# The order of SP's transfers written out by readiness, weight preparation moved to POOL, and squares taken from the moved tile

## The chip, the cores and the metric

The kernel runs on one core of one Trainium2 chip. The metric is the device time in microseconds. Three runs of the kernel before took 2990.77, 2992.46 and 3002.14 us; their median is 2992.46 us. A further, profiled execution took 2998.08 us, with a span of 2996.4 us from its first to its last instruction.

The engines are named as in the profile: PE (TensorE), PEld (its weight loads), DVE (VectorE), ACT (ScalarE), POOL (GpSimd) and SP (SyncE, which issues all transfers here). SPq is SP's instruction queue.

## The reference

Four transformer layers with a residual each, on x of 2048 rows by 512. Layers 0 and 2 are causal attention over a window of 256 keys with the weights A; layers 1 and 3 are full attention with the weights B. All have 32 heads of 16.

```python
def layer(x, wqkv, wo, windowed):
    q, k, v = heads(layernorm(x) @ wqkv)          # 32 heads of 16
    s = einsum("qd,kd->qk", q, k) * 16 ** -0.5    # for each head
    if windowed:
        s = where((i - j >= 0) & (i - j < 256), s, -1e9)
    return x + merge(softmax(s) @ v) @ wo

for windowed, w in ((True, A), (False, B), (True, A), (False, B)):
    x = layer(x, *w, windowed)
```

## The kernel before, in words

`fast_path` (line 189) holds the work. A layer is cut into four quarters of 512 rows (index `c`). Its steps are: load x, statistics and norm on DVE (`stats`, `norm`), transposes on PE (`transpose`), projections to queries, keys and values (`project`, `values`), attention, and the output projection with the residual (`wo`, or `wo_part` in layer 3).

Matrices are kept as two float16 parts, a high and a low one, so a projection of 128 columns is twelve matmuls (`mms`, line 382; the planner counts 0.222 per matmul). `project` (line 456) takes each bank of results `ps` out of PSUM as `sp`: the high part at line 479 on ACT (481 on DVE in the full layers), the low part at line 482 on DVE. Line 485 squares `ps` on ACT a second time out of PSUM; in the full layers line 487 squares the high part on POOL. The squares feed a bound on the scores that replaces the row maximum (`keys`, `queries`, `key_shift`). Queries and keys go to DRAM (`qs`, `kw`, `kf`) and are loaded back four heads (a `qd`) at a time: `load_win` (698) and `load_full` (686) load `qt`, two buffers, and `kt`, three. The eight `qd` of a quarter are the inner loop; in layer 3 the outer loop takes two `qd` at a time through all four quarters, so it has sixteen such passes.

Attention (`attn_win`, `attn_full`) makes scores on PE (line 673), exponentials on ACT (677), in the window layers the edges of the band by selects on POOL (739 and 742), and after two more steps (`flush(2)`) the products with the values on PE (717 and 749). A step of the full layers is one key tile for four heads, sixteen to a `qd`; the window layers have three to a `qd`.

`epilogue` (609) closes four heads. DVE copies the accumulator to `oe` (617), the denominators go to `lt` and the sums to `scr` in DRAM (622, 623). For every second `qd`, `reciprocals` runs later: it inverts `lt` (633), stores it (`rcp`, 635), loads the sums (`o`, 640) and the broadcast reciprocals (`r`, 641). Later still `normalised` multiplies them on DVE (644) and splits the product into `oh` (646, 647). The low part is taken on POOL in the full layers.

The weights of layer 0's projections are prepared at the start. The other five (`prep`, 338) are prepared during layer 0's attention. `maxima` (275) reduces each matrix's magnitudes over four row blocks in one DVE instruction (284); PE transposes the result (289). `scales` makes powers of two, and `parts` (319) scales each of four blocks (326, POOL), takes the high part (332, DVE for these five; 330, ACT, at the start) and the low part (333, POOL), and stores both in DRAM as `wd`. `weights` (367) loads them for each use into one of two buffers.

The order on PE is the order of the program (`manual_schedule`, line 202, names PE alone). On every other engine, SP among them, the compiler orders instructions by its own estimate of when their inputs are ready, with the order of the program as the priority. The program itself is laid out by a planner that counts a clock (`clock`, `spent`). `attention` (899) traces a step, then lets `Side` (818) put in pieces of projection, preparation and so on in proportion to the steps; line 876 aims to have them done two of its steps before the end of the quarter. A side step follows each window step and every second full step. What must come later waits in `pend` or `late` until the clock has reached a due time.

Of the kernel before, what the change touches and what calls it, by code (L numbers as in the profile page):

```python
# [188 lines left out]
def fast_path(ctx, tc, flag, a_x, a_wqkv, a_wo, b_wqkv, b_wo, out):  # L189
# [12 lines left out]
    ctx.enter_context(tc.manual_schedule(engines={mybir.EngineType.PE}))  # L202
# [5 lines left out]
    CM, DN, WT, ST, LN, pend = {}, {}, {}, {}, {}, []  # L208

    clock, DONE, ONR = [0.0], {}, {}  # L210

    def spent(us):
        clock[0] += us
        return us
# [60 lines left out]
    def maxima(ty, s, raw, ahead):  # L275
# [6 lines left out]
        if ahead:  # L282
            am = vp.tile([P, D], F32, name=f"wa{n}", tag="o")
            nc.vector.tensor_reduce(am, raw.rearrange("p k f -> p f k"), axis=AX.X, op=ALU.max,
                                    apply_absolute_value=True)
            yield
            pt = bank(f"wt{n}").rearrange("p (t f) -> p t f", f=P)
            for t in range(NHT):
                nc.tensor.transpose(pt[:, t, :], am[:, t * P:(t + 1) * P], ident)
            nc.vector.tensor_reduce(cm, pt, axis=AX.X, op=ALU.max)  # L290
            return
# [6 lines left out]
    def scales(ty, s):  # L298
# [7 lines left out]
        for v, name in ((up, "u"), (dn, "d"))[0 if s == 3 else 1:]:  # L306
            dg = vp.tile([P, NHT, P], F32, name=f"{name}g{n}", tag="oe")
# [11 lines left out]
    def parts(ty, s, raw, act):  # L319
# [3 lines left out]
        for k in range(NC + 1):  # L323
# [3 lines left out]
            if k:  # L327
# [3 lines left out]
                else:  # L331
                    nc.vector.tensor_copy(hi, r)
# [5 lines left out]
    def prep(ty, s):  # L338
        raw = load_w(ty, s)
        yield wait(14)  # L340
        for _ in maxima(ty, s, raw, True):
            yield wait(8 if s == 3 else 6)
# [24 lines left out]
    def weights(ty, s, n, t=None):  # L367

        w = wp.tile([P, NC, 2, D], F16, name=f"w{n}", tag="w", bufs=WB)
        if t is None:  # L370
            nc.sync.dma_start(w, wd[ty, s])
            return w
        nc.sync.dma_start(w[:, :, :, :P], wd[ty, s][:, :, :, t * P:(t + 1) * P])
# [46 lines left out]
    def load_x(l, c):  # L420
        xs = []
        for i in range(4):
            k = 4 * c + i
            x = vp.tile([P, D], F32, name=f"x{l}_{k}", tag="x", bufs=XB)
            nc.sync.dma_start(x, a_x[0, k * P:(k + 1) * P, :] if l == 0 else xd[k])
            xs.append(x)
# [29 lines left out]
    def project(l, s, c, act, w=None, ht=None):  # L456
# [3 lines left out]
        if not w:  # L460
            w = weights(ty, s, n, ht)
            yield wait(8)
        xc = XC[l, c]
# [7 lines left out]
        for t in range(NHT) if ht is None else (ht,):  # L471
# [3 lines left out]
            settle(not sqs)  # L475
            sp = vp.tile([P, 2, QC], F16, name=f"sp{n}_{t}", tag="sp", bufs=3)
# [7 lines left out]
            if act:  # L484
                nc.scalar.activation(sq, ps, AF.Square, scale=e)  # L485
# [4 lines left out]
            d = dst[8 * t:8 * t + 8].rearrange("h (d b) n -> (h d) b n", b=4)  # L490
            if s:
                nc.sync.dma_start(d[:, 0:2], sp[:, 0:1].broadcast_to([P, 2, QC]))
                nc.sync.dma_start(d[:, 2], sp[:, 1])
            else:
                nc.sync.dma_start(d[:, 0:2], sp)
                nc.sync.dma_start(d[:, 2], sp[:, 0])
# [25 lines left out]
    def queries(l, c, act, w=None, ht=None):  # L522
        sqs = yield from project(l, 0, c, act, w, ht)

        def rest():
            ph = squares(f"q{l}_{c}_{ht}", sqs)

            m = vp.tile([P, QC], F16, name=f"m{l}_{c}_{ht}", tag="m", bufs=1)
# [7 lines left out]
            for t in sqs:  # L536
                nc.sync.dma_start(rows(qs[l % 2, c])[8 * t:8 * t + 8, 3, :], m[32 * t:32 * t + 8, :])
# [6 lines left out]
    def key_shift(l, ht=None):  # L544
# [4 lines left out]
        nc.vector.tensor_reduce(kx[r], KM[l][r], axis=AX.X, op=ALU.max)  # L549
        m = vp.tile([P, QC], F16, name=f"mk{l}_{ht}", tag="m", bufs=1)  # L550
        nc.vector.tensor_scalar(m[r], ones[r], kx[r], -0.515, op0=ALU.mult, op1=ALU.mult)
        for t in range(NHT) if ht is None else (ht,):
            nc.sync.dma_start(rows(kf)[8 * t:8 * t + 8, 7, :].rearrange("h (c n) -> h c n", n=QC),
                              m[32 * t:32 * t + 8, None, :].broadcast_to([8, NQ, QC]))

    def values(l, c, act, w=None):
        n = f"{l}_{c}"
        if not w:
            w = weights(l % 2, 2, f"v{n}")
            yield wait(8)  # L560
        xc = XC[l, c]
# [13 lines left out]
    def wo(l, c):  # L575

        w = weights(l % 2, 3, f"o{l}_{c}")
        yield wait(8)

        xs = load_x(l, c)  # L580
        for i in range(4):
# [5 lines left out]
            nc.vector.tensor_add(xs[i], xs[i], d)  # L587
            nc.sync.dma_start(xd[k], xs[i])
            stats(l + 1, c, i, xs[i])
            yield -MM if PH["full"] else -12 * MM  # L590

    def wo_part(c, t):
# [6 lines left out]
        for i in range(4):  # L599
# [5 lines left out]
            nc.vector.tensor_add(xs[i], xs[i], d)  # L605
            nc.sync.dma_start(out[0, k * P:(k + 1) * P, :] if t == NHT - 1 else xd[k], xs[i])
            yield -MM

    def epilogue(l, c, qd, a, act):
        n = f"{l}_{c}_{qd}"  # L610
        t, u = divmod(qd, 2)
        oe = vp.tile([P, QC], F32, name=f"oe{n}", tag="oe")
# [5 lines left out]
        if u == 0:  # L618
            EP["scr"] = dp.tile([8, 32, QC], F32, name=f"scr{n}", tag="scr", bufs=4)
# [483 lines left out]
```

## Time and profile before

| what | value |
|---|---|
| median of three runs | 2992.46 us |
| profiled execution | 2998.08 us, span 2996.4 us |
| DVE, POOL and ACT busy in 85 to 600 us (most of layer 0) | 268.71, 248.82 and 260.98 us |
| transfers issued by SP | 395.92 MB |
| exponentials (line 677) | 2432 instructions, 1109 ns mean |

The stages: the first weights and projections up to some 85 us, layer 0 (window) to about 614 us, layer 1 (full) to about 1610, layer 2 (window) to about 2015, layer 3 (full) to about 2967, and the last output rows.

In a row of the timeline stand start, duration, engine, line, operation, and the tiles written and read. Brackets at the end hold the idle time of the engine before it and what ended that. In a row of waits stand the engine and line, what it waited for, the total, the number of times and the longest. In a row of groups: busy time and mean nanoseconds, then the idle time just before. A program with 16 DMA engines behind one issuing engine has two delays to a transfer: SP may not come to its instruction, and the data takes time to land.

### The profile page before, as it was taken

Reading aid. Unit: us, or ns where it says so; the run is one execution under the profiler, and the core shown is the slowest. Engines: PE = TensorE matmul, PEld = TensorE weight load, DVE = VectorE, ACT = ScalarE, POOL = GpSimd, SP = SyncE. Lnnn points to the kernel's source line nnn. Section 1 sums busy time; section 2 is a strip of 40 time slices with the busy share of each in tenths; the row PEclk is TensorE's granted clock in tenths of the full one; section 3 lists DMA queues with packets and bytes.
Section 4 is the critical chain, followed back from the end, with each engine's and each line's share of the span. In section 5 each row is a group of like instructions: output and inputs, shape, how many; then the busy total and the mean of one; then the engine's idle time right before and its main releaser. Section 6 shows DMA issues by size and latency. Waiting matters only on the chain.

```text
span 2996.4 us, 51979 instructions
## 1 busy us (share of the span) xinstructions
PE 2757.5 (92%) x20314; PEld 751.0 (25%) x20314; DVE 895.1 (30%) x1866; ACT 2402.0 (80%) x2703; POOL 557.5 (19%) x1127
## 2 busy tenths in 40 slices
PE   6787898899999999999999888789999999999996
PEld 3233333321122112212222333331211221112111
DVE  7665544401112113111212545531221222122212
ACT  3454555389999999999997666429999999999996
POOL 2546554100000000000002566500000000000000
PEclk8899999999999999999999999889999999999998
DMA  6575675532223232222323656432343333433332
GB/s 223 194 240 195 208 226 178 171 108 97 77 87 102 94 104 93 96 84 88 108 88 124 211 188 184 147 117 84 123 128 127 120 120 128 129 121 121 119 113 68
DMA packets 291408, 399.34 MB, mean 133 GB/s; under 512 B 70352, under 2 KB 173264, under 8 KB 283856
## 3 DMA queue, kind: packets, MB, share of 16 engines
q1 hardware_dynamic: 291152, 395.92, 40.6%
q8 instruction: 161, 2.64, 0.4%
q14 instruction: 95, 0.78, 0.1%
HBM read 263.19 MB, written 131.60 MB: 132 GB/s over the span
## 4 chain that ended last, share of the span: by engine, by line
PE 65%; ACT 10%; DVE 9%; DMA 9%; issue 4%; POOL 2%; SPq 1%; ACTq 0%; DVEq 0%; POOLq 0%
PE acc L717 25%; PE s L673 18%; PE acc L387 9%; ACT e L677 9%; PE pq L387 4%; PE pv L387 4%; DMA r<-rcp 4%; DMA rcp<-lt 3%; PE po L387 2%; PE acc L749 2%; DVE xh L417 1%; DMA scr<-oe 1%; DVE o L644 1%; DVE xh L414 1%; DVE xn L414 1%
## 5 line engine op out<-in xcount | busy, mean ns | idle before, releaser
L677 ACT ACTIVATE e<-s 128x1024 f32<-128x1024 f32 (+2 forms) x2432 | 2244.8, 1109 | 184.1 <-PE s L673 179.2
L717 PE MATMUL acc<-e,vt 128*17 128x512 f32 x8192 | 1078.6, 598 | 3.1 <-DVE oe L617 3.0
L673 PE MATMUL s<-qt,kt 64*128 64x512 f16 (+3 forms) x5504 | 798.7, 357 | 83.7 <-ACT e L677 14.2
L673 PEld LDWEIGHTS <-kt 64*128 64x128 f16 x5504 | 218.9, 94 | 944.9 <-issue 915.6
L742 POOL TENSOR_SCALAR_AFFINE_SELECT e<-e 128x256 f32<-128x256 f32 x512 | 223.7, 444 | 209.1 <-ACT e L677 208.4
L617 DVE COPY oe<-acc 128x512 f32<-128x512 f32 x128 | 88.1, 688 | 516.2 <-PE acc L717 461.9
L647 POOL TENSOR_TENSOR oh<-o,oh 128x512 f16<-128x512 f32 x32 | 37.1, 1159 | 1079.8 <-DVE oh L646 1079.8
L717 PEld LDWEIGHTS acc<-e,vt 128*17 128x17 f32 x8192 | 136.4, 95 | 351.1 <-issue 323.9
L739 POOL TENSOR_SCALAR_AFFINE_SELECT e<-e 128x256 f32<-128x256 f32 x448 | 194.3, 439 | 143.1 <-ACT e L677 140.6
L387 PE MATMUL pq<-xc,w 128*128 128x512 f16 x816 | 198.3, 397 | 12.6 <-ACT e L677 5.6
L749 PE MATMUL acc<-e,vt 128*17 128x384 f32 (+2 forms) x2816 | 204.3, 400 | 1.3 <-POOL e L739 1.1
L387 PEld LDWEIGHTS <-w 128*128 128x128 f16 x1152 | 106.2, 100 | 250.3 <-issue 157.8
L644 DVE TENSOR_TENSOR o<-o,r 128x512 f32<-128x512 f32 x64 | 53.2, 832 | 368.2 <-DMA r<-rcp 368.0
L387 PE MATMUL po<-wo,oh 128*128 128x512 f16 x444 | 113.9, 413 | 46.0 <-DVE dx L586 29.3
L479 ACT ACTIVATE sp<-pq,es 128x512 f16<-128x512 f32 x68 | 46.7, 687 | 108.6 <-PE pq L387 82.6
L387 PE MATMUL pv<-wv,xc 128*128 128x512 f16 x576 | 131.8, 385 | 1.5 <-ACT sq L485 0.6
L487 POOL TENSOR_TENSOR sq<-sp 128x512 bf16<-128x512 f16 x28 | 29.1, 1039 | 558.9 <-DVE sp L481 558.9
L387 PEld LDWEIGHTS <-oh 128*128 128x128 f16 x768 | 69.2, 101 | 213.3 <-issue 138.8
L570 ACT ACTIVATE vt<-pv 128x512 f32<-128x512 f32 x52 | 31.1, 597 | 110.1 <-PE pv L387 110.1
L387 PEld LDWEIGHTS <-xc 128*128 128x128 f16 x768 | 70.5, 99 | 140.7 <-issue 70.0
L481 DVE TENSOR_SCALAR sp<-acc,es 128x512 f16<-128x512 f32 x28 | 21.0, 750 | 268.2 <-PE acc L387 247.8
L387 PE MATMUL acc<-xc,w 128*128 128x512 f16 x336 | 95.4, 386 | 3.7 <-DVE sp L482 3.7
(128 smaller groups left out, 1486.3 us busy)
## 6 DMA issues: line engine op xcount, KB each, us to landing
kt<-kf SPq DMA_DIRECT2D x128, 512.0 KB
qt<-qs SPq DMA_DIRECT2D x128, 256.0 KB
scr<-oe SPq DMA_DIRECT2D x128, 256.0 KB
xd<-x SPq DMA_DIRECT2D x96, 256.0 KB
x<-xd SPq DMA_DIRECT2D x96, 256.0 KB
w<-wd SPq DMA_DIRECT2D x22, 1024.0 KB
kt<-kw SPq DMA_DIRECT2D x64, 256.0 KB
o<-scr SPq DMA_DIRECT2D x64, 256.0 KB
```

The source lines that it names most:

```text
L387: nc.tensor.matmul(ps, a, b, start=(i == 0), stop=(i == len(pairs) - 1))
L414: norm1 = lambda o: nc.vector.tensor_scalar(o, xs[i], mv[:, i, 0:1], y[:, i:i + 1], op0=ALU.subtract, op1=ALU.mult)
L479: nc.scalar.activation(sp[:, 0], ps, AF.Copy, scale=e)
L617: nc.vector.tensor_copy(oe, a)
L644: nc.vector.tensor_tensor(o, o, r, ALU.mult)
L647: (nc.gpsimd if l % 2 else nc.vector).tensor_tensor(ohl[:, 1], o, ohl[:, 0], ALU.subtract)
L673: nc.tensor.matmul(ps[:, h, s0:s0 + wd_], kt[R * h:R * h + R, pr, kc:kc + P], qt[R * h:R * h + R, pr, qc:qc + wd_], start=True, stop=True)
L677: nc.scalar.activation(e[:, :, w0:w1], ps[:, :, w0:w1], AF.Exp, scale=SCALE)
L717: nc.tensor.matmul(a[32 * h:32 * h + DH + 1, :], V[l, j // 4][:, j % 4, 4 * qd + h, :], es_[h // 2][:, h % 2, :], start=(j == 0), stop=(j ...
L739: nc.gpsimd.affine_select(v, v, pattern=[[0, 2], [-1, P]], compare_op=ALU.is_gt, fill=0.0, base=0, channel_multiplier=1)
L742: nc.gpsimd.affine_select(v, v, pattern=[[0, 2], [1, P]], compare_op=ALU.is_ge, fill=0.0, base=0, channel_multiplier=-1)
L749: nc.tensor.matmul(a[32 * h:32 * h + DH + 1, q * P:(q + nb) * P], V[l, (4 * c + j) // 4][:, j % 4, 4 * qd + h, :], es_[h // 2][:, h % 2, s ...
```

## The change

SP joins PE in `manual_schedule`: its transfers enter the queue in the order of the program. So that this order follows readiness, most of them are no longer issued where they are written. `post` puts a transfer on a list with a due time, the clock plus a delay, and `run_posts` issues what is due, sorted by due time, whenever the clock moves. `need` issues at once the listed transfers that write a named destination, ahead of a transfer or instruction that reads it. `number` does the same for transfers that read a tile's old buffer when the buffer is to be used again.

```diff
-    ctx.enter_context(tc.manual_schedule(engines={mybir.EngineType.PE}))
+    ctx.enter_context(tc.manual_schedule(engines={mybir.EngineType.PE, mybir.EngineType.SP}))
...
+    def post(out_, in_, delay, dst=None, of=None):
+        serial[0] += 1
+        posts.append((clock[0] + delay, serial[0], out_, in_, dst, of))
+        run_posts()
+
+    def run_posts(test=lambda x: False):
+        go = sorted(x[:2] for x in posts if x[0] <= clock[0] or test(x))
+        by = {x[:2]: x for x in posts}
+        for k in go:
+            x = by[k]
+            posts.remove(x)
+            nc.sync.dma_start(x[2], x[3])
+
+    def need(*dst):
+        run_posts(lambda x: x[4] in dst)
+
+    def number(tag, bufs):
+        made[tag] = made.get(tag, 0) + 1
+        run_posts(lambda x: x[5] is not None and x[5][0] == tag and x[5][1] <= made[tag] - bufs)
+        return tag, made[tag]
+
     def spent(us):
         clock[0] += us
+        run_posts()
         return us
```

The delays, in units of the planner's clock: weight loads 1.5; the stores of `sp` 2.5 and 3.5 (for queries the single row block first); the bound's rows `m` 2.5; key shifts 1.5; stores of x 3.0 (2.5 in layer 3); `lt` and `scr` 2.0; `rcp` 1.5; `r` 4.0; `qt` and `kt` 1.0. In the full layers the second half of `kt` waits 17 units more when the four heads before were of the same pass. `reciprocals` is due 5 after the epilogue (4.5 before) and `normalised` 9 after that (8 before). The loads of x and of `o` are issued where they stand. The loads for a pass's first four heads are posted at its start, and `need` issues them right ahead of the first scores:

```diff
+        need(("qs", 1, c), ("kf",))
+        early = KL.get("n") == (l, c, qd - 1)
+        KL["n"] = (l, c, qd)
+        post(qt, qs[1, c][pair].rearrange("r p n -> p r n"), 1.0, ("qt", n))
...
-            nc.sync.dma_start(kt, kf[pair, :, v * S // 2:(v + 1) * S // 2].rearrange("r p n -> p r n"))
+            post(kt, kf[pair, :, v * S // 2:(v + 1) * S // 2].rearrange("r p n -> p r n"),
+                 1.0 + 17 * v * early, ("kt", n, v))
...
     def attn_full(l, c, qd, kt, qt, a):
+        need(("qt", f"{l}_{c}_{qd}"))
         for j in range(NT):
+            if j % 8 == 0:
+                need(("kt", f"{l}_{c}_{qd}", j // 8))
...
-            nc.sync.dma_start(r, rcp[:, None, :].broadcast_to([8, DH, QC]))
+            post(r, rcp[:, None, :].broadcast_to([8, DH, QC]), 4.0, ("r", l, c, t))
 
             def normalised():
+                need(("rcp", l, c, t))
+                need(("r", l, c, t))
```

In the preparation of the five later matrices the high part moves from DVE to POOL, and the maxima are taken in two halves, with a planned wait of 4 between pieces (6 or 8 before) and into another buffer:

```diff
-            am = vp.tile([P, D], F32, name=f"wa{n}", tag="o")
-            nc.vector.tensor_reduce(am, raw.rearrange("p k f -> p f k"), axis=AX.X, op=ALU.max,
-                                    apply_absolute_value=True)
-            yield
+            am = vp.tile([P, D], F32, name=f"wa{n}", tag="dn", bufs=2)
+            for h in range(2):
+                f = slice(h * D // 2, (h + 1) * D // 2)
+                nc.vector.tensor_reduce(am[:, f], raw[:, :, f].rearrange("p k f -> p f k"), axis=AX.X, op=ALU.max,
+                                        apply_absolute_value=True)
+                yield
...
-                    nc.vector.tensor_copy(hi, r)
+                    nc.gpsimd.tensor_copy(hi, r)
                 nc.gpsimd.tensor_tensor(lo, r, hi, ALU.subtract)
```

In `project`, where ACT takes the high part, ACT squares that part instead of the bank:

```diff
             if act:
-                nc.scalar.activation(sq, ps, AF.Square, scale=e)
+                nc.scalar.activation(sq, sp[:, 0], AF.Square)
```

More of the change, by code (lines that the diff above doesn't have):

```diff
@@ L341, in prep @@
         for _ in maxima(ty, s, raw, True):
[L342 removed]
+            yield wait(4)
         yield -spent(1.0)
@@ L648, in normalised @@
                 ONR[l, c, t] = clock[0] + 4
-            late.append((clock[0] + 8, normalised))
-        late.append((clock[0] + 4.5, reciprocals))
+            late.append((clock[0] + 9, normalised))
+        late.append((clock[0] + 5, reciprocals))
     def run_late(done=False):
```

74 lines of the change are left out of this document (46 added, 28 removed).

## The prediction

> **What bounds the kernel now.** I read the page's first part, then the busy time by stage, then PE's gaps in the timeline of each stage, and behind each gap the engine that PE waited for.
>
> ```profile
> span 2996.4 us, 51979 instructions
> PE 2757.5 (92%) x20314; PEld 751.0 (25%) x20314; DVE 895.1 (30%) x1866; ACT 2402.0 (80%) x2703; POOL 557.5 (19%) x1127
> ...
> 85.00:600.00 515.00, 438.14 (x3466) 184.15 (x3467) 268.71 (x549) 260.98 (x342) 248.82 (x528) 0.93 0.62 201
> 600.00:1610.00 1010.00, 981.93 (x6954) 208.79 (x6953) 169.84 (x379) 953.92 (x1032) 47.75 (x47) 1.00 0.28 93
> 1610.00:2015.00 405.00, 337.96 (x2975) 139.10 (x2974) 190.94 (x433) 215.21 (x267) 194.93 (x482) 0.92 0.55 172
> 2015.00:2967.00 952.00, 937.44 (x6657) 189.72 (x6660) 195.13 (x358) 944.82 (x1024) 45.48 (x42) 1.00 0.36 116
> ```
>
> The columns of the stage rows are stage, length, busy time of PE, PEld, DVE, ACT and POOL, granted clock, DMA share and GB/s. The two full-attention layers (600 to 1610 and 2015 to 2967) have nothing to give: PE is idle 28 of 1010 us in one, ACT 7 of 952 us in the other. What can move is in the two window layers, where PE is idle 77 of 515 us and 67 of 405 us and its clock falls to 0.93 and 0.92. There the question is what PE waits for.
>
> ```profile
> 125.88 0.40 PE L673 MATMUL s<-qt,kt 64*128 64x256 f16 x2 [3.70 <-DVE km L519]
> 142.20 0.44 PE L673 MATMUL s<-qt,kt 64*128 64x384 f16 x2 [3.71 <-ACT sq L485]
> 212.01 1.09 PE L289 MATMUL wt<-ident,wa 128*128 128x128 f32 x4 [5.51 <-DVE wa L284]
> 229.77 2.75 PE L387 MATMUL po<-wo,oh 128*128 128x512 f16 x12
> 240.44 4.84 PE L387 MATMUL po<-wo,oh 128*128 128x512 f16 x12 [6.39 <-DVE dx L586]
> 251.58 4.40 PE L387 MATMUL po<-wo,oh 128*128 128x512 f16 x12 [4.77 <-DVE dx L586]
> 367.81 4.31 PE L387 MATMUL po<-wo,oh 128*128 128x512 f16 x12 [5.47 <-DVE dx L586]
> ...
> 121.06 4.17 DVE L332 CAST w<-wr 128x512 f16<-128x512 f32 x3 [1.55 <-POOL wr L326]
> 139.41 1.36 DVE L332 CAST w<-wr 128x512 f16<-128x512 f32 x1 [2.26 <-POOL wr L326]
> ```
>
> A bracket holds the idle time before the row and what ended it. In five gaps (all but the one at 212.01) DVE was in the casts of the weight preparation, line 332, waiting for POOL's products between them; what PE wanted (km, sp for the squares, dx) was queued behind. The five are 3.70 + 3.71 + 6.39 + 4.77 + 5.47 = 24.04 us. PE also comes back slow: the twelve matmuls that take 2.75 us at 229.77 take 4.84, 4.40 and 4.31 us behind three of them, 5.3 us more. So the casts cost **29.3 us**, all in layer 0.
>
> **The change part by part.** All sums are against the profiled execution, 2998.08 us with a span of 2996.4; the median of the runs shown is 2992.46, 5.6 lower. I carry the differences over to the median.
>
> *Weights on POOL alone.* Twenty casts leave DVE and twenty copies of the same shape join POOL.
>
> ```profile
> L332 DVE CAST w<-wr 128x512 f16<-128x512 f32 x20 | 26.8, 1369 | 14.1 <-POOL wr L326 14.1
> L326 POOL TENSOR_TENSOR wr<-wr,wd 128x512 f32<-128x512 f32 x20 | 26.9, 1364 | 1.2 <-ACT wd L317 1.2
> ...
> 141.95 0.41 POOL L742 TENSOR_SCALAR_AFFINE_SELECT e<-e 128x256 f32<-128x256 f32 x1
> 244.58 0.59 POOL L739 TENSOR_SCALAR_AFFINE_SELECT e<-e 128x256 f32<-128x256 f32 x1
> 370.72 0.40 POOL L739 TENSOR_SCALAR_AFFINE_SELECT e<-e 128x256 f32<-128x256 f32 x1
> ...
> 134.41 1.93 ACT L677 ACTIVATE e<-s 128x1024 f32<-128x1024 f32 x2
> 232.97 1.94 ACT L677 ACTIVATE e<-s 128x1024 f32<-128x1024 f32 x2 [2.40 <-PE s L673]
> 361.26 1.94 ACT L677 ACTIVATE e<-s 128x1024 f32<-128x1024 f32 x2 [2.40 <-PE s L673]
> 256.42 1.94 ACT L677 ACTIVATE e<-s 128x1024 f32<-128x1024 f32 x2 [8.76 <-PE s L673]
> 260.83 1.93 ACT L677 ACTIVATE e<-s 128x1024 f32<-128x1024 f32 x2
> ```
>
> The trace has no copy of this shape on POOL. One input over 256 columns takes a select 0.41 us, so 512 take at least some 0.8; two inputs over 512 take 1.36. I take 1.0, nearer the one-input end. That is 20 us more on POOL (16 to 27). What is hidden: PE uses an exponential two steps after ACT makes it, and a step with side work takes 4.4 us (256.42 to 260.83). What is late next: the selects. Those for the exponentials of 134.41 start at 141.95, of 232.97 at 244.58, of 361.26 at 370.72, each behind POOL's share of the preparation. If the copies that belong to the same weights (eight, six and four) stand in front too, they start at about 150, 250.6 and 374.7; PE without its old gaps wants them at 143.2, 241.8 and 370.1. It waits 6.8 + 8.8 + 4.6 = 20 us there in place of 29.3. **Gain 10** (from 29, if the copies fit between the selects, to a loss of 11, if all 27 us lie on the path, which leaves 29 - 27 = 2, and DVE is held up twice more by a busier POOL, 6.3 us each as below).
>
> ```profile
> 1872.76 7.05 DVE L644 TENSOR_TENSOR o<-o,r 128x512 f32<-128x512 f32 x1 [3.71 <-DMA r<-rcp]
> 1880.39 0.77 DVE L647 TENSOR_TENSOR oh<-o,oh 128x512 f16<-128x512 f32 x1
> ```
>
> A product of two SBUF tiles that takes under 0.8 us elsewhere took 7.05 us here, while selects ran on POOL back to back. The Trainium skill, page "SBUF — State Buffer", section "Who interferes with whom", says why it may be: DVE's second SBUF input comes through a port pair shared with GpSimd, and whichever starts first holds it for its whole instruction. The same rule would explain casts of 1.37 us, and it speaks on both sides: the moved copies stop fighting DVE's casts, and lengthen the time in which DVE's products and differences are blocked. By it alone the term could lie anywhere between the two ends above; the sum stays with the rows.
>
> *Maxima in two halves.* The gap at 212.01 is a reduction of 3.61 us that PE's transposes wait for. Halved, other DVE work can pass between; the transposes follow the second half, at a later due time. I take **4** of the 5.5 us; nothing excludes 0.
>
> *Squares from the moved first part.*
>
> ```profile
> ACT sq L485 <- DVE sp L482: 28.7, 19, 5.1
> PE s L673 <- ACT sq L485: 8.2, 7, 3.7
> PE phk L504 <- ACT sq_h L485: 2.1, 1, 2.1
> ...
> L485 ACT ACTIVATE sq<-pq,es 128x512 bf16<-128x512 f32 x68 | 47.1, 693 | 38.2 <-DVE sp L482 38.1
> ```
>
> ACT's square now waits until DVE has read the same bank, and holds the bank for another 0.69 us. From sp it needs ACT's own copy only, and the bank is free when DVE is done. Each time PE waited for a square (seven times before scores, and eight more in smaller rows of both layers, the last of them before phk) it may go on up to 0.69 us earlier: 15 x 0.69 = 10, of which one is counted with the casts. ACT's 38 us of waiting goes too, but ACT is not the limit there. The square itself reads SBUF instead of PSUM: no row for it, I take the same 0.69. **Gain 8** (0 to 14).
>
> *The order of SP's queue.* Here the trace shows the cause of waits, not the new order.
>
> ```profile
> DVE o L644 <- DMA r<-rcp: 368.0, 61, 11.3
> ...
> 316.91 4.16 PE L387 MATMUL pq<-xc,w 128*128 128x512 f16 x12 [1.81 <-ACT sq L485]
> 1894.35 5.28 PE L387 MATMUL po<-wo,oh 128*128 128x512 f16 x12 [7.85 <-DVE dx L586]
> 1926.85 4.44 PE L387 MATMUL pq_h<-xc,w_h 128*128 128x512 f16 x12 [2.86 <-DVE xc L450]
> ...
> 1893.00 0.69 DVE L644 TENSOR_TENSOR o<-o,r 128x512 f32<-128x512 f32 x1 [6.27 <-DMA r<-rcp]
> ```
>
> DVE stands still 368 us before the normalisation until the broadcast reciprocals land. In the full layers PE does not notice. In the window layers seven gaps of PE, from 316.91 to 1926.85, have such a stall right in front (6.27 us at 1893.00 ahead of PE's 7.85): 24 us, with 8 us of slow restarts. The change posts r four units after rcp, so SP no longer stands in front of it, and traces the normalisation 1.5 units later in all; DVE's work can pass if the compiler's order follows. Against that, r itself is issued no earlier. I take a third, **gain 10** (0 to 32).
>
> The price: SP now runs in the order of the program. The loads of a quarter's first four heads are written at the quarter's start and forced out right before its first scores.
>
> ```profile
> 2045.92 0.38 SPq L690 DMA_DIRECT2D qt<-qs  x1
> 2076.37 0.62 SPq L622 DMA_DIRECT2D lt<-oe  x1
> ...
> 2977.13 0.61 SPq L641 DMA_DIRECT2D r<-rcp  x1
> 2980.67 0.69 DVE L644 TENSOR_TENSOR o<-o,r 128x512 f32<-128x512 f32 x1 [7.71 <-DMA r<-rcp]
> ```
>
> In the kernel before, that load is issued as soon as it can be: this qt of layer 3's second quarter goes out at 2045.92, and the first quarter's last heads, still running then, are only stored at 2076.37, some 5 us after the second begins; a lead of about 25 us. 256 KB take 3.5 us from issue to use (2977.13 to 2980.67); qt with 512 KB of kt I put at 4.4 us, an estimate from that row. That is hidden if SP is over 4.4 us ahead of PE. The side work of a quarter is planned to end two of its steps early, about 7 us in a full layer and 5 to 9 in a window layer; less 2.5 us until the last store is due, SP has about 4.5 us. The 20 starts in full layers I take as hidden, and of the 8 in window layers, where side work runs late, two uncovered: **loss 8** (0 to 28 x 4.4 = 123). Weight loads, stores and x loads are posted when they can run; I count them at nothing, since the side work has 1.5 to 4 units of slack, and at the same 4.4 us a time if it has not.
>
> **Sum**: -10 - 4 - 8 - 10 + 8 = -24 us; 2998 - 24 = 2974 for the profiled execution, **2968 us** against the median.
>
> **The rivals.**
> *The order is worth more.* All of the 32 us at the r stalls goes and no start of a quarter waits: -24 - 22 - 8 = -54, **2938**. For it: the stall is in nearly every normalisation, 61 of 64. Against: r has the same three transfers in a row.
> *POOL takes it all back.* The copies sit on the path and the order changes nothing: 0 - 4 - 8 + 8 = -4, **2988**. For it: at 141.95 and 244.58 selects already stand behind the preparation. The lock that the Trainium skill's page tells of, above, would help it.
> *Slower: the first loads of each quarter come too late.* In all 28 starts PE stands until qt and kt have landed, 4.4 us less SP's lead. The other terms save 32, so it decides against the change from 28 x (4.4 - lead) = 32, a lead of 3.3 us, and costs over 0.5% from a lead of 2.7 on (47 us). At a lead of 2 it is 67 - 32 = +35: **3027**; at 2.5, **3014**. For it: in before the same loads go out some 25 us early, and in program order any late store ahead of them delays them. Against: two scores' tiles are stored up for ACT, and the side work has the two steps.
>
> **How the numbers follow.** Forecast 0.42, more from the order 0.17, POOL takes it back 0.16, slower 0.25. About 0.5%, 15 us, is what a measurement of this kernel can tell from no change. Faster by more: 0.17 and nearly all of the forecast, 0.58; within: 0.17; slower: 0.25. The range is 2932 to 3014: it leaves out half of the slower case and a little of the best.
>
> **What would show it.** Right: no casts on DVE in layer 0's preparation and twenty POOL copies of 0.8 to 1.4 us; PE's gaps before dx, km and squares of 120 to 370 us replaced by shorter waits for selects; fewer and shorter DVE waits for r in the window layers; full layers as long as before. Wrong: waits of PE's scores for qt or kt where a quarter begins, most of all 16 of them in the last layer; a layer 0 that is no shorter; DVE waits for r as long as now, which would mean that the compiler's order did not follow.

## The result, and the profile after

The changed kernel takes 3024.43 us (median of four runs, 3021.35 to 3026.68) against 2993.31 for the kernel before (four runs): ratio **1.0096** [1.0079, 1.0114], some 29 us slower (the two medians lie 31 us apart). 2968 was forecast, with a range that ended at 3014.

The engine line and the costliest group of PE, from the page of the kernel after:

```profile
span 3019.6 us, 51979 instructions
...
PE 2756.6 (91%) x20314; PEld 748.2 (25%) x20314; DVE 892.0 (30%) x1851; ACT 2399.6 (79%) x2703; POOL 571.4 (19%) x1147
...
L722 PE MATMUL s<-qt,kt 64*128 64x512 f16 (+3 forms) x5504 | 793.8, 358 | 112.5 <-DMA kt<-kw 43.2
```

PE works as long as before (2756.6 us, 2757.5 before); what grew is its idle time. The two stretches of the window layers (columns as before; they begin and end at the same times as before, though the layers moved), then the products with the values of the two window layers before and after, which give the layers' own length:

```profile
85.00:600.00 515.00, 425.80 (x3386) 175.19 (x3386) 268.59 (x521) 254.17 (x333) 262.68 (x548) 0.91 0.62 205
...
1610.00:2015.00 405.00, 339.40 (x3069) 134.82 (x3068) 185.83 (x425) 231.29 (x283) 196.88 (x486) 0.93 0.53 170
```
```profile
L749 PE MATMUL acc<-e,vt x1408: 272/379/847, 88.1 to 542.4; 128*17 128x384 f32 x63, 128*17 128x128 f32 x57, 128*17 128x256 f32 x56
L749 PE MATMUL acc<-e,vt x1408: 272/379/847, 1617.1 to 1941.7; 128*17 128x384 f32 x64, 128*17 128x256 f32 x56, 128*17 128x128 f32 x56
```
```profile
L807 PE MATMUL acc<-e,vt x1408: 272/390/847, 89.8 to 563.7; 128*17 128x384 f32 x62, 128*17 128x128 f32 x58, 128*17 128x256 f32 x56
L807 PE MATMUL acc<-e,vt x1408: 272/390/844, 1641.4 to 1968.2; 128*17 128x384 f32 x64, 128*17 128x256 f32 x56, 128*17 128x128 f32 x56
```

Layer 0 went from 454.3 to 473.9 us, layer 2 from 324.6 to 326.8. Of the 23.2 us between the two spans, layer 0 alone holds 19.6. Layer 2 is only 2.2 us longer, although PE waits 15.2 us there for late loads (4.25, 7.49 and 3.44 us, below): the change gains something in that layer too. What PE waits for, over the whole kernel, in the view of waits (total, times, longest):

```profile
PE s L722 <- DMA kt<-kw: 43.2, 10, 7.5
...
PE po L419 <- DVE m_None L573: 15.8, 1, 15.8
PE acc L807 <- POOL e L797: 13.5, 8, 6.6
...
PE s L722 <- DMA kt<-kf: 6.7, 12, 1.2
```

Before, PE waited for no kt from kw. Of the 43.2 us after, 6.42 stand at the very first scores (86.68 us), where PE before waited 5.46 us for qt; they are no loss of the change. Where the larger others are, in the timeline of PE: at the second four heads of layer 0, and then at the first scores of a quarter. Each window layer has three quarters behind its first; five of the six starts stand here, the sixth comes next.

```profile
104.22 0.82 PE L722 MATMUL s<-qt,kt 64*128 64x384 f16 x4 [5.50 <-DMA kt<-kw]
198.26 1.03 PE L722 MATMUL s<-qt,kt 64*128 64x128 f16 x8 [6.83 <-DMA kt<-kw]
339.98 0.61 PE L722 MATMUL s<-qt,kt 64*128 64x128 f16 x8 [2.97 <-DMA kt<-kw]
458.06 1.03 PE L722 MATMUL s<-qt,kt 64*128 64x128 f16 x8 [3.34 <-DMA kt<-kw]
...
1807.70 0.61 PE L722 MATMUL s<-qt,kt 64*128 64x128 f16 x8 [4.25 <-DMA kt<-kw]
...
1916.97 0.61 PE L722 MATMUL s<-qt,kt 64*128 64x128 f16 x8 [3.44 <-DMA kt<-kw]
```

The first qt of each of these five starts on SP's queue:

```profile
193.31 0.38 SPq L228 DMA_DIRECT2D qt<-qs  x1
...
335.63 0.41 SPq L228 DMA_DIRECT2D qt<-qs  x1
...
453.17 0.40 SPq L228 DMA_DIRECT2D qt<-qs  x1
...
1801.36 0.38 SPq L228 DMA_DIRECT2D qt<-qs  x1
...
1911.34 0.38 SPq L228 DMA_DIRECT2D qt<-qs  x1
```

The start of the second quarter of layer 2, with SP's queue in front of it, first after, then the same start before:

```profile
1712.69 0.84 PE L807 MATMUL acc<-e,vt 128*17 128x384 f32 x8
1712.87 0.62 SPq L228 DMA_DIRECT2D r<-rcp  x1
...
1713.55 0.96 SPq L228 DMA_DIRECT2D kw<-sp  x2
...
1714.61 0.58 SPq L228 DMA_DIRECT2D lt<-oe  x1
...
1715.82 0.39 SPq L228 DMA_DIRECT2D qt<-qs  x1
...
1721.02 1.04 PE L722 MATMUL s<-qt,kt 64*128 64x128 f16 x8 [7.49 <-DMA kt<-kw]
```
```profile
1681.35 0.41 SPq L703 DMA_DIRECT2D qt<-qs  x1
...
1689.99 0.39 PE L673 MATMUL s<-qt,kt 64*128 64x128 f16 x4
```

Before, SP issues qt 8.6 us ahead of the scores (1681.35 to 1689.99). After, PE has nothing left at 1713.5, SP is still at r, the stores and lt, and qt goes out at 1715.82: 2.3 us after PE needed it. PE starts 5.2 us after that issue. At the six starts the issue lies between 2.3 us behind and 2.2 us ahead of the moment at which PE has nothing left (1.9 behind, 1.4 and 1.6 ahead in layer 0; 2.3 behind, 2.1 and 2.2 ahead in layer 2), and PE starts 4.4 to 6.3 us after it.

The longest single gap of PE in layer 0 stands behind one instruction. DVE, POOL and PE after:

```profile
262.42 16.30 DVE L693 TENSOR_TENSOR o<-o,r 128x512 f32<-128x512 f32 x1 [4.44 <-DMA r<-rcp]
...
278.03 0.96 POOL L800 TENSOR_SCALAR_AFFINE_SELECT e<-e 128x256 f32<-128x256 f32 x1
...
280.70 1.86 PE L419 MATMUL po<-wo,oh 128*128 128x512 f16 x4 [15.77 <-DVE m_None L573]
```

A product that takes 0.69 us elsewhere lasted until POOL, busy throughout, paused; the output projection stood behind it for 15.77 us.

### The profile page after: what moved, and what is told of

The parts are those of the page before. It is cut to its first block, busy times and chain, and to the rows that moved or that the text cites. A ratio compares the mean times of both kernels' runs of the same rounds, so it can differ in the third digit from the quotient of the medians.

```text
span 3019.6 us, 51979 instructions
## 1 busy us (share of the span) xinstructions
PE 2756.6 (91%) x20314; PEld 748.2 (25%) x20314; DVE 892.0 (30%) x1851; ACT 2399.6 (79%) x2703; POOL 571.4 (19%) x1147
## 4 chain that ended last, share of the span: by engine, by line
PE 65%; DMA 11%; DVE 9%; ACT 7%; issue 3%; SPq 2%; POOL 2%; ACTq 0%; DVEq 0%; POOLq 0%
PE acc L775 25%; PE s L722 17%; PE acc L419 9%; ACT e L726 7%; PE pq L419 4%; PE pv L419 3%; PE acc L807 3%; DMA r<-rcp 3%; DMA kt<-kf 3%; DMA rcp<-lt 2%; PE po L419 2%; DMA kt<-kw 1%; SPq L228 1%; DMA scr<-oe 1%; DVE o L693 1%
## 5 line engine op out<-in xcount | busy, mean ns | idle before, releaser
L722 PE MATMUL s<-qt,kt 64*128 64x512 f16 (+3 forms) x5504 | 793.8, 358 | 112.5 <-DMA kt<-kw 43.2
L661 DVE COPY oe<-acc 128x512 f32<-128x512 f32 x128 | 88.2, 689 | 595.9 <-PE acc L775 493.7
L807 PE MATMUL acc<-e,vt 128*17 128x384 f32 (+2 forms) x2816 | 214.8, 410 | 13.6 <-POOL e L797 13.5
L693 DVE TENSOR_TENSOR o<-o,r 128x512 f32<-128x512 f32 x64 | 64.8, 1012 | 327.9 <-DMA r<-rcp 324.8
```

Of the source, the lines that this page charges most:

```text
L661: nc.vector.tensor_copy(oe, a)
L693: nc.vector.tensor_tensor(o, o, r, ALU.mult)
L722: nc.tensor.matmul(ps[:, h, s0:s0 + wd_], kt[R * h:R * h + R, pr, kc:kc + P], qt[R * h:R * h + R, pr, qc:qc + wd_], start=True, stop=True)
L807: nc.tensor.matmul(a[32 * h:32 * h + DH + 1, q * P:(q + nb) * P], V[l, (4 * c + j) // 4][:, j % 4, 4 * qd + h, :], es_[h // 2][:, h % 2, s ...
```

## The experiments

Each time is compared with the kernel before, run in turn on the same chip (3002 to 3004 us in these runs; a ratio of 0.001 is 3 us). Kernels are compared with each other by these ratios. Layer lengths are those of the profile, one or two for each kernel, from first to last product with the values.

### The parts alone

**e1_squares**: before, with `activation(sq, sp[:, 0], AF.Square)` as in the change.

> The kernel before with the squares of line 485 taken from the moved high part, nothing else. Every theory expects a small gain: the prediction's 8 us, so a ratio of 0.997 (0.995 to 1.000) against the kernel before, and no wait of PE for ACT's squares.

Measured: 1.0013 [1.0001, 1.0025], a loss of 4 us, though the interval almost reaches 1; the gain that every theory expected is not there. The waits of PE for DVE's low part, and the same place in e1 and in before:

```profile
PE s L673 <- DVE sp L482: 21.7, 8, 4.6
```
```profile
313.43 0.69 ACT L479 ACTIVATE sp<-pq,es 128x512 f16<-128x512 f32 x1 [1.28 <-PE pq L387]
...
314.92 0.63 ACT L485 ACTIVATE sq<-sp 128x512 bf16<-128x512 f16 x1
...
316.72 0.76 DVE L644 TENSOR_TENSOR o<-o,r 128x512 f32<-128x512 f32 x1 [5.35 <-DMA r<-rcp]
...
318.76 0.74 DVE L482 SCALAR_TENSOR_TENSOR sp<-pq,es,sp 128x512 f16<-128x512 f32 x1
319.55 0.71 PE L673 MATMUL s<-qt,kt 64*128 64x128 f16 x6 [4.62 <-DVE sp L482]
```
```profile
312.80 0.40 PE L673 MATMUL s<-qt,kt 64*128 64x128 f16 x4 [0.21 <-DMA kf<-sp]
...
315.40 0.74 DVE L482 SCALAR_TENSOR_TENSOR sp<-pq,es,sp 128x512 f16<-128x512 f32 x1
```

The square is early now, but the bank is not free: DVE's low part stands behind the normalisation, which waits for r. Before, the next scores ran at 312.80 without that bank and the next projection waited 1.81 us for it (row of 316.91 above); in e1 the scores are what takes it, and PE waits 4.62 us. The wait passed from ACT to DVE and from a projection to the scores.

**e2_prep**: before, with the preparation as changed (copies on POOL, maxima in halves, waits of 4).

> The kernel before with the preparation part alone: high part on POOL, maxima in two halves, waits of 4. Theory 'late first loads' (the change loses its time at the starts of the window layers' quarters, and the preparation gains as predicted): 10 to 25 us faster, ratio 0.992 to 0.997. Theory 'POOL' (the longer preparation on POOL holds back selects and blocks DVE's products of two tiles, as the 16.3 us product at 262 us of the changed kernel shows): no gain, ratio 0.999 to 1.005, with single DVE products of over 5 us in 100 to 400 us.

Measured: 0.9971 [0.9957, 0.9985], 9 us gained, at the edge of the first theory's range. No product in layer 0 lasts over 3 us. **e5_act**: the same, with the copies on ACT.

```diff
-                    nc.gpsimd.tensor_copy(hi, r)
+                    nc.scalar.activation(hi, r, AF.Copy)
```

> The kernel before with the preparation's part of the change (maxima in halves, shorter planned waits) and the twenty copies on ACT instead of POOL. With the copies on POOL this part alone had measured 0.9971, some 9 us gained, where the casts on DVE had cost 29.3 us. Theory 'POOL takes most of it back': the copies in front of the selects are what ate the rest, so here PE's waits for POOL's selects (20.8 us in 14 waits with the copies on POOL) fall back to under 8 us and the ratio is 0.990 to 0.995, 2964 to 2978 us on a chip where the kernel before takes 2993. Theory 'the gaps were only moved' (DVE was late anyway, ACT gets 20 more instructions of some 0.6 us in a stage in which its exponentials are needed): 0.996 to 1.000, and PE waits for ACT in place of POOL.

Measured: 0.9960 [0.9947, 0.9973]. Waits of PE in e2, then in e5:

```profile
PE acc L751 <- POOL e L741: 20.8, 14, 8.1
```
```profile
PE s L675 <- ACT e L679: 24.6, 42, 5.7
...
PE acc L751 <- POOL e L741: 2.9, 7, 1.0
```

The wait for the selects falls as the first theory said (20.8 to 2.9 us), and the wait for ACT's exponentials takes half of its place (14.8 us in 37 waits in e2). The two intervals overlap: which engine makes the copies is worth little.

**e3_order**: after, with squares and preparation as before, so the order of SP's queue alone.

> The changed kernel with squares and preparation put back, so SP's order alone. Theory 'late first loads': 20 to 35 us slower than before, ratio 1.007 to 1.012, with waits of PE for kt of some 35 us in the window layers. Theory 'POOL': within 8 us of before, ratio 0.997 to 1.003.

Measured: 1.0117 [1.0095, 1.0139], 35 us lost: the order, with its list and its later due times, is the loss. Kt again leads the new waits, 40.2 us in 12.

### First loads, and who orders SP

**e4_early**: after, with a window quarter's first loads written as soon as its keys and queries are projected.

```diff
-                ops = load(l, c, qds[0])
+                ops = KL.pop("first", None) or load(l, c, qds[0])
...
+                            if (qd == qds[-1] and c + 1 < NQ and "first" not in KL and not pend
+                                    and all((x, l, c + 1) in DONE for x in "KQ")):
+                                KL["first"] = load(l, c + 1, qds[0])
```

> The changed kernel, but in the window layers the loads for a quarter's first four heads are posted as soon as its keys and queries are projected, during the last four heads of the quarter before. Theory 'late first loads': 25 to 35 us less than the changed kernel, about 2990 us, and no wait of PE for kt at six of the eight starts. Theory 'POOL': at most 10 us less than the changed kernel, 3014 or more.

Measured: 1.0015 [0.9998, 1.0032], 24 us better than after, just short of what the first theory gave, and some waits at the starts stay. Kt's waits halve (7.0 of what is left is at the very first scores), and DVE's long product is not there, at the place where it was:

```profile
PE s L722 <- DMA kt<-kw: 23.9, 6, 7.0
```
```profile
261.91 0.69 DVE L693 TENSOR_TENSOR o<-o,r 128x512 f32<-128x512 f32 x1 [2.67 <-DMA r<-rcp]
```

So e4 took away two things, the late loads by its edit and the 15.8 us by its timing. **e6_free** leaves everything as changed but the order: `manual_schedule(engines={mybir.EngineType.PE})`.

> The changed kernel with one thing undone: SP is not in the manual order, so the compiler orders SP's transfers by its own estimate again, with the new order of the program as its priority. All postponed transfers, the later due times of reciprocals and normalisation, the preparation and the squares stay as changed. Theory 'late first loads, because SP runs in program order': the waits of the scores for kt and qt at the starts of quarters are nearly gone (kt of the window layers from 43.2 us to under 12), and the ratio to the kernel before is that of preparation and squares together, 0.996 to 1.001. Rival 'the postponement itself': the posts come late in the program, the compiler's order follows the program, and the later due times of the normalisation cost too: the waits stay above 30 us and the ratio is 1.007 to 1.012.

Measured: 1.0021 [1.0008, 1.0033], 22 us better than after, just above the range of the first theory and far below the rival's, and kt is gone from the larger waits. **e13_post** is e6 with the squares from PSUM again.

> The changed kernel with SP's order left to the compiler and the squares taken from PSUM again; the list of due times, the later due times of the normalisation and the preparation on POOL stay. With the squares as changed it had 1.0021; preparation alone 0.9971, squares alone 1.0013. Theory 'the parts add up, and the later places in the program cost some 11 us': 1.0008. Theory 'the order costs only because it is fixed': then with the compiler's order only the preparation is left, 0.996 to 0.998, and squares cost more beside the later due times than alone.

Measured: 0.9974 [0.9962, 0.9985], as e2's 0.9971. The list of due times and the later normalisation cost nothing, and gain nothing, as long as the compiler orders SP; squares cost 14 us there (0.9974 to 1.0021), not 4. The parts do not simply add. This tests the list only under the compiler's order, where DVE waits for r in the window layers as long as before (141.7 us, 133.8 before).

**e12_prog**: before, with SP in `manual_schedule` and nothing else.

> The kernel before with one thing changed: SP in the manual order, its transfers in the order in which the program of the kernel before writes them, with no list of due times. Theory 'a fixed order of SP makes loads late, and the list of due times repairs most of it': stores are written right after the step that makes their data, so SP stands in front of each, loads behind them come later than in the changed kernel, and it is slower than 1.012 (the fixed order with the list of due times alone): 1.015 to 1.08. Rival 'the list itself makes the loads late': without it the loads are written early and the ratio is under 1.010.

Measured: 1.0369 [1.0344, 1.0395], 111 us lost. The list repairs some two thirds of what a plain program order costs.

### What else the fixed order costs

**e14_nosq** is after with the squares from PSUM, **e9_early_nosq** the same with early first loads, **e15_again** after once more.

> The changed kernel with one thing undone: the squares are taken from PSUM again. If squares cost 14 us wherever they stand (1.0021 against 0.9974 with the compiler's order): 1.0049. If the sum of the parts alone holds (order 1.0117, preparation 0.9971): 1.0088. If squares cost nothing under a fixed order: 1.0096.

> The changed kernel with the window layers' first loads written early and the squares taken from PSUM again; preparation as changed. Chain of single steps so far: preparation 0.9971, with the list of due times and the compiler's order of SP 0.9974, with the squares 1.0021, with SP's order fixed 1.0096, with early first loads 1.0015. Theory 'late first loads are the whole cost of the fixed order, and the squares cost 14 us wherever they stand': 0.996 to 0.998, as good as the preparation alone. Rival 'the fixed order has a second cost of some 11 us that the squares only hid': 1.000 to 1.003 (the kernel with copies on ACT instead had 1.0028).

> The changed kernel once more, for a second profile. If the product of 16.3 us on DVE in layer 0, with PE's 15.8 us gap behind it, belongs to this kernel's timing, it is there again at about 262 us, at 10 us or more; if it is chance, the longest such product is elsewhere or under 4 us, and the profiled time is some 10 us shorter than 3021. The late first loads of the window quarters (6.8, 3.0, 3.3, 7.5, 4.3 and 3.4 us) are there in either case, within 1.5 us each.

Measured: e14 1.0096 [1.0062, 1.0131], e9 1.0038 [1.0018, 1.0058], e15 3032.43 us in its one run (3002.48 before). e9 lies above both ranges that were given for it, nearer to the rival's. Between after and e14 the squares cost nothing. In e15 all six late starts are there again, each within 0.6 us. The long product is in all three; e15's row, and the gap of PE behind it:

```profile
261.63 15.46 DVE L693 TENSOR_TENSOR o<-o,r 128x512 f32<-128x512 f32 x1 [4.95 <-DMA r<-rcp]
...
279.16 3.15 PE L419 MATMUL po<-wo,oh 128*128 128x512 f16 x7 [15.49 <-DVE m_None L573]
```

It lasts 16.16 us in e14 and 15.36 in e9: it belongs to this timing and is not chance. It is not the fixed order's alone: with the compiler's order it lasts 12.79 us in e6 and 11.25 in e13. There PE stands 7.78 and 7.03 us behind it, against 15.90 in e9, so under the fixed order that gap is some 8 to 9 us longer. **e17_after_act** shortens it in the changed kernel by copies on ACT (diff as e5), **e18_early_act** does that and early first loads; **e8_best** is e18 with the squares from PSUM.

> The changed kernel with one thing else: the twenty copies of the preparation on ACT instead of POOL, so that POOL pauses for each. In four profiles with the copies on POOL and SP's order fixed to the list, one DVE product of layer 0 lasted 15.4 to 16.3 us, while POOL worked 17 us without a pause, and PE stood 15.5 to 16.3 us behind it. Theory 'the unbroken run of POOL is the second cost': no DVE product over 8 us, no gap of PE for m_None, waits of the scores for kt still 40 us or more, and the ratio falls from 1.0096 by about 16 us to 1.003 to 1.006. Rival 'PE's other waits fill the place': the gap goes, ACT's copies cost as much, and the ratio is 1.008 to 1.011.

> The changed kernel with early first loads and with the copies on ACT, squares as changed: both costs that the profiles show are taken away. With early first loads alone it had 1.0015, and there the long product was absent already (0.7 us) while PE waited 16.3 us for POOL's selects. Theory 'late first loads and POOL's run are the whole loss': 0.996 to 1.000. Rival 'a fixed order costs more than these two': 1.001 to 1.004, as the same kernel with the squares from PSUM had (1.0028).

> The changed kernel with the window layers' first loads written early (as in the run with early first loads, 1.0015 against the kernel before), the squares taken from PSUM again (their part alone had measured +4 us) and the twenty copies on ACT. Theory 'late first loads', with the parts adding up: 1.0015 less 0.0013 for the squares, less what the copies on ACT gain over those on POOL (0 to 20 us): 0.994 to 1.000. Theory 'POOL': the copies are the main loss, and the ratio falls to 0.992 or lower. If the parts do not add up it stays at 1.001 to 1.003.

Measured: e17 1.0074 [1.0049, 1.0098], e18 1.0005 [0.9988, 1.0022], e8 1.0028 [1.0011, 1.0044]. In e17:

```profile
265.37 5.09 DVE L693 TENSOR_TENSOR o<-o,r 128x512 f32<-128x512 f32 x1 [4.55 <-DMA qs<-sp]
...
272.36 4.13 PE L419 MATMUL po<-wo,oh 128*128 128x512 f16 x12 [5.58 <-DVE m_None L573]
```

The waits for kt stay (41.7 us). PE's gap falls by 10 us (15.8 to 5.6), the time by 7, between the two theories, and the intervals of after and e17 overlap. Also, with copies on ACT two new waits of PE for DVE's low part appear in layer 0 (5.90 us at 149.12 and 4.70 at 253.51), so e17 does not take out the gap alone, and its price is not settled. Early first loads, in three pairs that differ in nothing else, are worth 24 us (after and e4), 17 (e14 and e9) and 21 (e17 and e18). In two pairs with early first loads that differ only in the squares (e9 and e4, e8 and e18), the changed squares are 7 us the better, though the intervals of each pair overlap.

**e11_soon** is e4 with no delay on the window layers' loads of qt and kt and on all weight loads (`post(..., 0.0, ...)`).

> The kernel with early first loads (1.0015 against the kernel before) with one thing more: the window layers' loads of qt and kt and all weight loads enter SP's queue with no delay (1.0 and 1.5 units in the change). Of the order's cost of some 35 us about 11 is left there, and PE still waits 23.9 us for kt in the window layers, 5 to 7 us of it at each of three places in layer 0, and 2 to 2.5 us for the output weights three times. Theory 'what is left are also late loads': these waits fall to under 12 us together and the ratio is 0.997 to 1.000. Rival 'it is the later due times of the normalisation and the stores in front': the waits stay and the ratio is 1.001 to 1.004.

Measured: 1.0048 [1.0031, 1.0064], 10 us worse than e4 and above both ranges. The waits in the window layers did not go (25.9 us), and new ones came in the full layers, where e4 had 9.0 us in 13:

```profile
PE s L722 <- DMA kt<-kf: 20.6, 15, 3.0
```

### DVE beside POOL, by itself

**e7_port**, **e10_port2** and **e16_port3** leave out the whole computation and time single DVE instructions of 128x512 while POOL works without a pause. In e7 the compiler ordered POOL, so its runs became selects and products in turn; in the others the order is fixed.

> Leaves out the whole computation: it copies x to the output and times single DVE instructions of 128x512 alone and beside back-to-back runs of POOL instructions on other tiles (24 or 48 selects, 8 products of two SBUF tiles, 16 copies to float16). Theory 'a DVE product of two SBUF tiles does not come in between two POOL instructions' (as the 16.3 us product in layer 0 of the changed kernel suggests): the product lasts about as long as the POOL run beside it, 10 us or so beside 24 selects, 20 beside 48, while one with an input in PSUM stays under 1 us. Rival 'it shares with POOL by turns' (at most the wait for one instruction): at most 2 us in every case, whatever the length of the run. For a cast or a product with a number (one SBUF input) the first theory leaves it open: alone under 0.6 us; beside the run either the same or as long as the run.

> Leaves out the whole computation: it copies x to the output and times single DVE instructions of 128x512 beside runs of POOL instructions, this time in a fixed order on both engines, so that the DVE instruction starts just as a POOL instruction of the run does. In the first such kernel every DVE product of two SBUF tiles took 0.87 us beside POOL's work, and it always began beside a select; one cast to float16 that met four POOL products took 6.07 us. Theory 'whoever holds the way to SBUF first keeps it, run after run': the product beside 8 POOL products (9 us) lasts about as long as the run, beside 4 about half as long, beside selects under 1 us, and the cast beside 8 products 8 to 10 us; the product with an input in PSUM stays at 0.7. Rival 'by turns': none above 2.5 us, the wait for one POOL instruction. If only mixed runs (product, copy, difference, selects, as in the weight preparation) hold a product for long, the 16.3 us product of the changed kernel needs that mixture.

> Leaves out the whole computation: it copies x to the output and times a DVE product of two SBUF tiles and a DVE cast to float16, ten times each, beside six POOL selects and six POOL products in turn (9 us), each time begun at another moment by a piece of other DVE work of 0.1 to 0.7 us in front. In a fixed order beside runs of one kind all of them ended within 1.51 us; in the first such kernel, beside selects and products in turn, one cast took 6.07 us and another begun alike 1.69. Theory 'the start decides': most end within 1.6 us, and some, begun while a product runs, last until POOL pauses, 5 us or more. Rival 'by turns, and the one cast was a slip of the record': all 20 under 2.5 us.

In DVE's timeline, e10's product beside eight products of POOL (beside selects it took 0.87 us), and e7's cast:

```profile
36.67 1.51 DVE L94 TENSOR_TENSOR d_tt_mule<-g_tt_mule,ta 128x512 f32<-128x512 f32 x1 [4.38 <-POOL g_tt_mule L89]
```
```profile
47.91 6.07 DVE L86 CAST d_castmul<-g_castmul 128x512 f16<-128x512 f32 x1 [1.53 <-POOL g_castmul L77]
```

All 20 of e16 and all 14 of e10 ended within 1.61 us, also beside product, copy, difference and selects as in the preparation (1.51); with an input in PSUM 0.69. Only e7's cast lasted until POOL paused. What lets a product through here and not in layer 0 stays open.

## Why the prediction was wrong, point by point

- **Where the time lies** was right. Full layers are as long as before (990.8 and 990.9 us in layer 1, 951.2 and 952.3 in layer 3, from first to last product with the values); all that moved moved around the window layers.
- **Weights on POOL alone**, gain 10 with 20 us of waits for selects in place of 29: right alone in the mechanism: in e2 PE waits 20.8 us for selects. The copy took less than the least that was thought (next row, against 0.8 to 1.36). With the maxima in halves, gain 4, the two terms make 14; e2 measured 9 for both together (the interval gives 4 to 13), and no run splits them. PE's wait for wa, 5.5 us before, is gone in e2. What the sum did not hold is the long product of layer 0: it lasts over 11 us in five of the seven kernels that have both the list and the copies on POOL, and 5.1 to 6.7 us in the three with the list and the copies on ACT; in before, e1, e2, e3 and e5 no product of layer 0 lasts over 3 us.

```profile
L364 POOL CAST w<-wr 128x512 f16<-128x512 f32 x20 | 13.1, 667 | 0.0
```

- **Squares**, gain 8 (14 times 0.69 is 9.7; the text does not say how it becomes 8): wrong in sign. "The bank is free when DVE is done" is true, but DVE is done late, behind r, and another PE instruction takes the bank. A loss of 4 us alone, 14 with the list, none between after and e14; with early first loads it looks like a gain of 7.
- **Order, gain at the r stalls**, 10: the waits fell as foreseen, and the sum of the change hides what they are worth. DVE's wait for r in the window layers fell from 133.8 to 88.2 us (83.1 in e3), and the output projection's wait for dx behind it from 29.3 to 2.1 us (3.2 in e3, where the casts are still on DVE). The rows are those of layer 2 (1610 to 2015 us), before and after. The gain shows where the late loads are taken away: layer 2 lasts 315 to 320 us in the five kernels with early first loads, against 324.6 before and 325.9 to 327.9 in e2, e5 and e13. That is 5 to 13 us, from one profile for each kernel.

```profile
DVE o L644 <- DMA r<-rcp: 74.5, 16, 9.4
```
```profile
DVE o L693 <- DMA r<-rcp: 50.8, 15, 7.9
```

- **Late first loads**, loss 8: this is the step that failed. "SP has about 4.5 us" of lead was worked out from the planner's slack, and two of eight window starts were taken as uncovered. SP's place in its queue was not in that sum: SP comes to the load only after r, which waits for rcp, and after the stores of `lt` and `scr`. Its lead is -2.3 to 2.2 us at the six starts, and the load takes 4.4 to 6.3 us from issue to use, where the estimate had 4.4. So all six starts behind a window layer's first quarter wait, 6.83 + 2.97 + 3.34 + 7.49 + 4.25 + 3.44 = 28.3 us in place of 8, and early loads give back 17 to 24. That the 20 starts of the full layers are hidden was right: 6.7 us in 12 waits, 1.2 at most.
- **Weight loads**, counted at nothing: PE's waits for `wo` rose from 2.4 us in one to 6.9 in three. The fourth, 13.68 us at the last output rows, stands where PE before waited 12.62 us for `oh`.
- **The rival that had the time**, slower because first loads come late, is shown as the largest cause, but not as it was priced: not 28 starts at 1.9 to 2.4 us each (4.4 less a lead of 2.5 or 2), but six at 3.0 to 7.5. That its 3014 to 3027 holds the measured time is in part luck: it set 53 to 67 us of waits against 32 us of savings, of which the squares' 8 did not come.
- **What stays open.** With the squares as changed, early first loads bring the fixed order back to the compiler's (e4 1.0015, e6 1.0021); with the squares from PSUM, 19 us are left (e9 1.0038, e13 0.9974). The profiles put this rest into layer 0 (468.1 us in e9, 442.1 in e13; layer 2 is shorter in e9, 316.3 against 325.9). Of it the longer gap behind the long product is 8 to 9 us. Another piece is in every kernel with early first loads: at 217 to 227 us PE stands 7 to 9 us for DVE's low part, or for the square behind it, while DVE first does the maxima and a norm. e13 has no wait of over 4 us for these. The rows are of e4 and of e9, where DVE's order was read. That these two make up the rest is not shown by a run. The kernels with early loads still wait 19 to 24 us for kt, 6 to 7 of it at the very first scores, and e11, meant to end that, made it worse. Why the squares cost 14 us in one order and nothing in the other was not found.

```profile
227.41 0.61 PE L722 MATMUL s<-qt,kt 64*128 64x384 f16 x4 [8.13 <-DVE sp L518]
```
```profile
219.35 0.58 PE L541 MATMUL phk_None<-sq,hsum 128*32 128x512 bf16 x1 [8.85 <-ACT sq L521]
```

The quickest kernel of all is e5, the preparation alone with its copies on ACT: 0.9960 [0.9947, 0.9973], 12 us better than before, with neither the order nor the squares. Its interval overlaps those of e2 and e13.

## What to carry to other kernels

A queue that runs in program order does each transfer when everything written ahead of it has been waited for, as qt at 1715.82 behind r and the stores: before fixing such an order, read for each load how far ahead of its use it is issued now, and where the stores in front of it would put it. A wait that is taken off one engine must be followed to the next holder of the same buffer, here from ACT's square to DVE's low part. And parts measured alone need not add: squares cost 4, 14 and 0 us in three programs, and seem to gain 7 in two more.

## What the runs showed that was not expected

A DVE product of two SBUF tiles lasted 15.4 to 16.3 us in four profiles (after, e15, e14, e9), 12.79 in e6 and 11.25 in e13, 0.69 at the same place in e4, and at most 1.61 in 22 trials by itself. The Trainium skill, page "SBUF — State Buffer", section "Who interferes with whom", says that such a product shares a port pair with GpSimd and that the one that starts first holds it for its whole instruction. The trials agree (0.69 us alone, 1.51 behind one POOL product of 1.04). The 16.30 us do not: some 25 POOL instructions, none over 1.3 us, passed in that time.
